# Row scatters without an order among them, and weight casts tied to the turns of a scan

## The chip, the cores and the metric

The kernel runs on one core of one Trainium2 chip. The metric is the device time of one execution in microseconds. A timed run of the kernel before gives one number; the median of three such runs is its time. A profile of one further execution shows every instruction on the engines: TensorE (PE, with its weight loads PEld), VectorE (DVE), ScalarE (ACT), GpSimd (POOL) and SyncE (SP, which here only issues DMAs).

## The reference

Two stages. The first is a gated linear attention over batch 4, 8 heads, 768 steps and head size 48, with a complex gate whose modulus is cut at 0.999:

```
scale = minimum(mag, 0.999) / (mag + 1e-06)
new_re = ar * S_re - ai * S_im;  new_im = ar * S_im + ai * S_re
S_re, S_im = new_re + kv, new_im          # kv: outer product of k[t] and v[t]
y[t] = q[t] @ S_re
```

The second takes the 3072 x 384 rows of y as tokens x of a mixture of 8 experts, of which each token uses one:

```
logits = x @ w_gate + modality_bias[modality_id]
e = argmax(logits)
out[token] = softmax(logits)[e] * (relu(x[token] @ w1[e]) @ w2[e])   # 384 -> 1024 -> 384
```

## The kernel before

**The program and its order.** The kernel is written in a layer that records instructions in program order and then places them: each engine has one queue in a fixed order, chosen by a planner that steps through a simulated time and takes, for an engine that is free, the ready instruction that comes first in the program. The layer finds dependencies by the tiles and memory ranges that an instruction reads and writes and adds the semaphore waits. On the chip each engine then works through its queue in order, so a waiting instruction holds all that stand behind it.

**The gate loop** (`gate_loop`). The 32 (batch, head) pairs are cut into 8 stretches of 96 steps, 256 rows in all, treated in two rounds `r` of 128 rows, one row a partition. For each round `elem(r)` is the scan: it walks 12 chunks `c` of 8 steps from the last (`c` = 11) to the first. In each step DVE makes the complex product of the running gate product `e` and the normed gate `an` (tile `x`, line 143) and adds its parts (line 150). Beside it `modulus` loads the gates two chunks ahead (tile `ab`, SP, lines 66 and 67) and squares them on ACT (line 69), and `hats` squares a finished chunk's `e` (line 97), scales q and k by it, transposes q on TensorE (line 111) and writes k to the scratch `kh` in HBM (line 115).
`units(r)` is the attention itself: 16 units for a round, each with a `front` (load `KW` from `kh` and `V`, memsets of V and KT on POOL in lines 170 and 173, transposes of KW in line 177, scores `wp` in line 184 and their mask on DVE), a `decay` and a `back` (products `py`, the gate logits, and the bf16 rows to `x_rows` in HBM). Round 0's scan runs alone; round 1's is woven chunk by chunk between the units of round 0; the units of round 1 run alone.

**The weight casts** (`cast_weights`). Sixteen DMAs on POOL's queue turn the experts' f32 weights into bf16 copies `w1b` and `w2b` in HBM, 768 KB of output each (lines 289 and 290). They stand before the gate loop in the program and depend on nothing.

**The expert stage** (`moe_sorted`). The tokens are sorted by expert into tiles of 256 slots by a chain of DVE operations. For each tile `fetch` loads the expert's w1 and w2 from the bf16 copies (SP, lines 444 and 445, three buffers each) and gathers 256 rows of x_rows by two indirect DMAs on POOL (line 449, six buffers); `turn` transposes them; `up` makes the first layer (line 469) with relu on DVE and ACT; `down` makes the second layer (line 481), scales it into `y_sb` (line 484 on ACT, line 486 on DVE, four buffers) and scatters the 128 rows to `out` by an indirect DMA on POOL (line 487). Twelve tiles always run; those beyond stand in Ifs on the count found on the chip. In the profiled execution 13 tiles ran, 26 gathers and 26 scatters. All scatters write to `out` at rows known only on the chip, so the layer makes each wait for the one before.

Of the kernel before, what the change touches and what calls it, by code (L numbers as in the profile page):

```python
# [13 lines left out]
Alu = mybir.AluOpType  # L14
# [5 lines left out]
ET = mybir.EngineType  # L20


def gate_loop(nc, ctx, tc, cpool, ident, identb, q, k, v, a_re, a_im, wgp, x_rows, lg):


    B, H, S, D = q.shape
# [36 lines left out]
    def modulus(r, c, box):  # L63

        ab = st.tile([P, 2, T, D], F32, name="ab", bufs=3)
        nc.sync.dma_start(out=ab[:, 0], in_=rows(a_re, r, c))
        nc.sync.dma_start(out=ab[:, 1], in_=rows(a_im, r, c))
        sq = st.tile([P, 2, T, D], F32, name="sq")
        nc.scalar.activation(sq[:], ab[:], Act.Square)
        yield  # L70
        m = st.tile([P, T, D], F32, name="m", bufs=3)
        nc.vector.tensor_tensor(m[:], sq[:, 0], sq[:, 1], Alu.add)
        nc.scalar.activation(m[:], m[:], Act.Ln, scale=1.0 / (0.999 * 0.999))
        nc.scalar.activation(m[:], m[:], Act.Exp, scale=-0.5)
        g = st.tile([P, T, D], F32, name="g")
        nc.scalar.activation(g[:], m[:], Act.Copy, scale=-1e-6 / 0.999, bias=1.0)  # L76
        yield
        nc.vector.scalar_tensor_tensor(g[:], m[:], 1.0, g[:], Alu.min, Alu.mult)
        box[c] = (ab, g)

    def gates(c, box):

        ab, g = box[c]
        an = st.tile([P, T, 4, D], F32, name="an")
        nc.vector.tensor_tensor(an[:, :, 0:2, :].rearrange("p t c d -> p c t d"), ab[:], g[:, None].broadcast_to([P, 2, T, D]), Alu.mult)
        nc.scalar.activation(an[:, :, 2, :], an[:, :, 1, :], Act.Copy, scale=-1.0)
        nc.scalar.activation(an[:, :, 3, :], an[:, :, 0, :], Act.Copy)
        box[c] = an
# [28 lines left out]
    def elem(r):  # L117

        QT = qt.tile([C, P, L], F32, name="QT", bufs=2)
        for_round[r] = QT  # L120
        last = NCH - 1
        E = {last: st.tile([P, T, 2, D], F32, name="e", bufs=3)}
        nc.vector.memset(E[last][:, T - 1, 0, :], 1.0)
        nc.vector.memset(E[last][:, T - 1, 1, :], 0.0)
        cl = un.tile([P, 2, D], F32, name="cl", bufs=1)
        box = {}
        for c in (last, last - 1):
            for _ in modulus(r, c, box):
                pass
        gates(last, box)  # L130
        for c in range(last, -2, -1):
            hs = hats(r, c + 1, E.pop(c + 1), QT) if c < last else iter(())
            ms = modulus(r, c - 2, box) if c > 1 else iter(())
            next(hs, None)
            next(ms, None)
            beside = [None, hs, ms, hs, hs, ms, hs, ms]
            if c >= 0:
                an = box.pop(c)
                if c:
                    E[c - 1] = st.tile([P, T, 2, D], F32, name="e", bufs=3)  # L140
                for i in range(T - 1, -1, -1):
                    x = st.tile([P, 2, 2, D], F32, name="x")
                    nc.vector.tensor_tensor(x[:], E[c][:, i, :, None, :].broadcast_to([P, 2, 2, D]), an[:, i].rearrange("p (u w) d -> p u w d", u=2), Alu.mult)  # L143
                    if i == T - 1:
                        if c:
                            gates(c - 1, box)
                    else:
                        next(beside[T - 1 - i], None)
                    to = E[c][:, i - 1] if i else (E[c - 1][:, T - 1] if c else cl[:])
                    nc.vector.tensor_tensor(to, x[:, 0], x[:, 1], Alu.add)  # L150
            for g in (ms, hs):
                for _ in g:
                    pass
            if c == 0:
                nc.sync.dma_start(out=c_scr[r], in_=cl.rearrange("p c d -> p (c d)"))
            yield
# [105 lines left out]
    for _ in elem(0):  # L262
        pass
    for r in range(NR):
        us = units(r)
        if r + 1 < NR:

            es = elem(r + 1)
            n, m = NB * G, NCH + 1
            done = 0  # L270
            next(es)
            for i in range(n):
                next(us)
                while done * n < (i + 1) * (m - 1):
                    next(es)
                    done += 1
            for _ in es:
                pass
        for _ in us:
            pass  # L280


def cast_weights(nc, moe_w1, moe_w2):

    E, Dt, F = moe_w1.shape
    w1b = nc.dram_tensor("w1b", (E, 128, Dt // 128, F), BF16, kind="Internal").ap()
    w2b = nc.dram_tensor("w2b", (E, 128, F // 128, Dt), BF16, kind="Internal").ap()
    for e in range(E):
        nc.gpsimd.dma_start(out=w1b[e], in_=moe_w1[e].rearrange("(k p) f -> p k f", p=128))
        nc.gpsimd.dma_start(out=w2b[e], in_=moe_w2[e].rearrange("(c p) d -> p c d", p=128))  # L290
    return w1b, w2b


def moe_sorted(nc, ctx, tc, cpool, identb, lg, x_rows, w1b, w2b, moe_modality_id, moe_modality_bias, out):

    N, Dt = out.shape
# [140 lines left out]
    ids = mp.tile([128, NH], U32, name="ids")  # L437
# [38 lines left out]
    def down(i, w2t, hT):  # L476
        for s in range(HS):
            c = i * HS + s
            y_ps = pp.tile([128, Dt], F32, name="y_ps", tag="y", bufs=2)
            for f in range(NF):  # L480
                nc.tensor.matmul(y_ps[:], hT[:, f, s * 128:(s + 1) * 128], w2t[:, f, :], start=(f == 0), stop=(f == NF - 1))  # L481
            y_sb = fp.tile([128, Dt], F32, name="y_sb", bufs=4)
            if s % 2 == 0:
                nc.scalar.activation(y_sb[:], y_ps[:], Act.Copy, scale=inv[:, 1, c:c + 1])
            else:
                nc.vector.tensor_scalar(y_sb[:], y_ps[:], inv[:, 1, c:c + 1], None, Alu.mult)  # L486
            nc.gpsimd.indirect_dma_start(out=out, out_offset=bass.IndirectOffsetOnAxis(ap=ids[:, c:c + 1], axis=0), in_=y_sb[:], in_offset=None, bounds_check=N - 1, oob_is_err=False)  # L487


    got = fetch(0)  # L490
# [1 line left out]
    for i in range(NL):  # L492
        coming = fetch(i + 1)
        hT = up(got[0], xgT)
        if i + 1 < NL:
            xgT = turn(coming[2])
        down(i, got[1], hT)
        got = coming
    nt = nc.values_load(ntile[0:1, 0:1], min_val=NL, max_val=NS, skip_runtime_bounds_check_because="N tokens in at most E tiles that are not full")  # L499
    with ExitStack() as more:  # L500
        for i in range(NL, NS):
            more.enter_context(tc.If(nt > i))
            if i > NL:
                got = fetch(i, "n")
            down(i, got[1], up(got[0], turn(got[2])))


@with_exitstack
def kernel(
    ctx: ExitStack,  # L510
    tc: tile.TileContext,
    q: bass.AP,
    k: bass.AP,
    v: bass.AP,
    a_re: bass.AP,
    a_im: bass.AP,
    moe_modality_id: bass.AP,
    moe_w_gate: bass.AP,
    moe_modality_bias: bass.AP,
    moe_w1: bass.AP,  # L520
    moe_w2: bass.AP,
    out: bass.AP,
):
    nc = tc.nc
    B, H, S, D = q.shape
    N, Dt = out.shape
    E = moe_w_gate.shape[1]
    assert Dt == H * D

    x_rows = nc.dram_tensor("x_rows", (N, Dt), BF16, kind="Internal").ap()  # L530

    cpool = ctx.enter_context(tc.tile_pool(name="c", bufs=1))
    ident = cpool.tile([128, 128], F32, name="ident")
    make_identity(nc, ident[:])
    identb = cpool.tile([128, 128], BF16, name="identb")
    nc.vector.tensor_copy(identb[:], ident[:])
    lg = cpool.tile([96, N // 96, E], F32, name="lg")

    wgp = cpool.tile([128, H // 2, 32], F32, name="wgp")
    nc.vector.memset(wgp[:], 0.0)  # L540
    for u in range(2):
        nc.sync.dma_start(out=wgp[u * 64:u * 64 + D, :, 0:E], in_=moe_w_gate.rearrange("(j u d) e -> u d j e", u=2, d=D)[u])

    w1b, w2b = cast_weights(nc, moe_w1, moe_w2)
    with ExitStack() as gstack:
        gate_loop(nc, gstack, tc, cpool, ident, identb, q, k, v, a_re, a_im, wgp, x_rows, lg)
    moe_sorted(nc, ctx, tc, cpool, identb, lg, x_rows, w1b, w2b, moe_modality_id, moe_modality_bias, out)


# [28 lines left out]
```

## Time and profile before

| | |
|---|---|
| timed runs | 612.57, 619.71, 619.93 us (median 619.71) |
| profiled execution | time 614.6 us, span 612.7 us |
| mean granted TensorE clock | 0.851 |
| PE busy | 397.7 us (65% of the span) |
| DVE busy | 354.4 us (58%) |
| ACT busy | 266.7 us (44%) |
| POOL busy | 82.7 us (13%) |
| DMA moved | 91.49 MB, mean 149 GB/s |

The span runs from the first to the last instruction of the profiled execution; its time is 1.9 us longer. The shares are means over stages: the scan of round 0 up to about 125 us, scan and units together to about 315, the units of round 1 to about 445, the sort to about 483, the experts to the end. A granted clock of 1.00 is 2.4 GHz and one of 0.50 is 1.2 GHz; means between them mix the two. A DMA share is the mean busy share of 16 DMA engines; where packets overlap it can be above 1.

### The profile page before, as it was taken

The numbers are of one execution on the slowest core, as the hardware profiler recorded it, in microseconds if no ns is written. First come the engines' busy times: TensorE is split into PE (matmuls) and PEld (weight loads), VectorE is DVE, ScalarE is ACT, GpSimd is POOL, SyncE is SP. The second block draws the span as 40 slices with busy tenths as digits, with TensorE's granted clock in tenths as the row PEclk, the third lists the DMA queues.
The fourth block names the chain that finished last, engine by engine and source line by source line (L and its number), as shares of the span: only waits on it lengthen the run. The fifth ranks groups of instructions, "written<-read, shape, count | busy, mean of one in ns | idle before, by whom it ended". The sixth has DMA issues, their size and how long they took to land. (4 is left out here: it accounts for less than half of the span.)

```text
span 612.7 us, 10055 instructions
## 1 busy us (share of the span) xinstructions
PE 397.7 (65%) x3656; PEld 292.1 (48%) x3656; DVE 354.4 (58%) x884; ACT 266.7 (44%) x597; POOL 82.7 (13%) x144
## 2 busy tenths in 40 slices
PE   0022122129799978987987999999914695876670
PEld 0011011117566656665656767776604574654450
DVE  1899999988876587588871444444365142232120
ACT  3556756475745574476652444444410031211120
POOL 5112000000000000000000000000000343435322
PEclk9999999999755685588996999999955599887886
DMA  9999998365652364353525445444217177765610
GB/s 201 234 243 267 261 254 218 116 175 117 172 151 74 93 159 127 87 154 99 134 70 114 88 93 105 91 98 99 50 12 305 32 269 254 255 230 184 206 53 28
DMA packets 108405, 91.49 MB, mean 149 GB/s; under 512 B 73342, under 2 KB 97314, under 8 KB 108352
## 3 DMA queue, kind: packets, MB, share of 16 engines
q1 hardware_dynamic: 93920, 70.94, 41.7%
q0 software_dynamic: 14432, 19.86, 15.7%
q8 instruction: 31, 0.51, 0.4%
q14 instruction: 22, 0.18, 0.1%
HBM read 86.75 MB, written 29.59 MB: 190 GB/s over the span
## 5 line engine op out<-in xcount | busy, mean ns | idle before, releaser
L111 PE MATMUL tq<-ident,Qh 128*96 128x128 f32 x192 | 42.9, 390 | 119.2 <-DVE Qh L107 119.2
L111 PEld LDWEIGHTS tq<-ident,Qh 128*96 128x96 f32 x192 | 31.3, 180 | 128.2 <-ACT g L76 62.0
L219 PE MATMUL py<-KW,V 96*64 96x192 f32 x512 | 88.9, 378 | 0.0
L185 DVE TENSOR_TENSOR KW<-wp,mask 96x384 f32<-96x384 f32 x64 | 35.3, 553 | 78.5 <-PE wp L184 67.0
L143 DVE TENSOR_TENSOR x<-e,an 128x192 f32<-128x192 f32 x192 | 67.7, 353 | 2.5
L184 PE MATMUL wp<-QT,KT 96*64 96x96 f32 x1024 | 65.8, 287 | 0.8 <-ACT KT L178 0.5
L184 PEld LDWEIGHTS wp<-QT,KT 96*64 96x64 f32 x1024 | 58.5, 165 | 5.6 <-ACT KT L178 4.3
L469 PE MATMUL h_ps<-xgT,w1t 128*128 128x256 bf16 x312 | 42.6, 296 | 25.2 <-DVE hT L471 22.0
L473 ACT ACTIVATE hT<-h_ps 128x512 bf16<-128x512 f32 x26 | 15.5, 597 | 97.5 <-PE h_ps L469 97.5
L150 DVE TENSOR_TENSOR e<-x 128x96 f32<-128x96 f32 x190 | 48.0, 253 | 2.7
L469 PEld LDWEIGHTS <-w1t 128*128 128x128 bf16 x312 | 32.8, 105 | 33.3 <-issue 26.3
L173 POOL MEMSET KT<- 96x256 f32 x32 | 10.9, 365 | 275.0 <-PE wp L184 275.0
L223 PE MATMUL py<-QT,Zs 96*48 96x96 f32 x448 | 37.5, 272 | 14.1 <-ACT Zs L209 14.1
L177 PE MATMUL tk<-ident,KW 96*96 96x96 f32 x256 | 40.1, 298 | 9.4 <-DMA KW<-kh 8.9
L219 PEld LDWEIGHTS py<-KW,V 96*64 96x64 f32 x512 | 39.6, 154 | 10.4 <-issue 2.4
L486 DVE TENSOR_SCALAR y_sb<-y_ps,inv 128x384 f32<-128x384 f32 x13 | 8.0, 617 | 60.9 <-DMA out_dram<-y_sb,ids 48.0
L112 ACT COPY QT<-tq 96x512 f32<-96x512 f32 x48 | 27.5, 582 | 34.9 <-PE tq L111 34.7
L481 PE MATMUL y_ps<-w2t,hT 128*128 128x384 bf16 x208 | 40.5, 353 | 0.0
L223 PEld LDWEIGHTS py<-QT,Zs 96*48 96x48 f32 x448 | 26.7, 136 | 26.9 <-ACT Zs L209 22.7
L209 ACT COPY Zs<-tz 96x512 f32<-96x512 f32 x28 | 16.3, 582 | 48.5 <-PE tz L207 48.5
L177 PEld LDWEIGHTS tk<-ident,KW 96*96 96x96 f32 x256 | 28.5, 154 | 17.6 <-issue 10.4
L178 ACT COPY KT<-tk 96x384 f32<-96x384 f32 x64 | 29.2, 477 | 16.9 <-PE tk L177 16.1
(120 smaller groups left out, 700.6 us busy)
## 6 DMA issues: line engine op xcount, KB each, us to landing
w1t<-w1b SPq DMA_DIRECT2D x13, 768.0 KB, 5.0
w2t<-w2b SPq DMA_DIRECT2D x13, 768.0 KB, 5.5
kh<-e SPq DMA_DIRECT2D x24, 384.0 KB, 2.9
KW<-kh SPq DMA_DIRECT2D x32, 288.0 KB, 3.7
w1b<-in_moe_w_dram POOLq DMA_DIRECT2D x8, 768.0 KB, 43.8
w2b<-in_moe_w_dram POOLq DMA_DIRECT2D x8, 768.0 KB, 46.4
cB<-c_scr SPq DMA_DIRECT2D x56, 96.0 KB, 3.4
ab<-in_a_re_dram SPq DMA_DIRECT2D x24, 192.0 KB, 5.3
```

Source lines behind the costliest of these rows:

```text
L111: nc.tensor.transpose(tp[:, i, :], Qh[:, t4 + i].rearrange("p c d -> p (c d)"), ident[:])
L112: nc.scalar.copy(QT[:, :, c * T + t4:c * T + t4 + 4], tp.rearrange("c t p -> c p t"))
L143: nc.vector.tensor_tensor(x[:], E[c][:, i, :, None, :].broadcast_to([P, 2, 2, D]), an[:, i].rearrange("p (u w) d -> p u w d", u=2), Alu.mult)
L150: nc.vector.tensor_tensor(to, x[:, 0], x[:, 1], Alu.add)
L177: nc.tensor.transpose(tp[:, i, :], KW[:, h4 + i, 0:C], ident[:L, :L])
L178: nc.scalar.copy(KT[:, h4:h4 + 4, 0:L], tp[:])
L184: nc.tensor.matmul(wp[u * 64:(u + 1) * 64, i, :], KT[:, h4 + i, u * 64:(u + 1) * 64], QT[:, p, :], start=True, stop=True)
L185: nc.vector.tensor_tensor(KW[:, h4:h4 + 4, C:], wp[0:L], mask[:, None, :].broadcast_to([L, 4, L]), Alu.mult)
L219: nc.tensor.matmul(py[u * 64:(u + 1) * 64, i, :], V[:, 2 * j + u, :], KW[:, 2 * j + u, :], start=True, stop=(g == 0))
L223: nc.tensor.matmul(py[u * 64:u * 64 + D, i, C:], Zs[:, j, u * 64:u * 64 + D], QT[:, p, :], start=False, stop=True)
L469: nc.tensor.matmul(h_ps[:, f, :], w1t[:, k, ff * 128:(ff + 1) * 128], xgT[:, k, :], start=(k == 0), stop=(k == KD - 1))
L481: nc.tensor.matmul(y_ps[:], hT[:, f, s * 128:(s + 1) * 128], w2t[:, f, :], start=(f == 0), stop=(f == NF - 1))
```

## The change

Two parts. The scatters to `out` are put into a group whose members are declared to have no dependency on each other: they write rows of different tokens. And the sixteen casts are no longer issued ahead of the gate loop; `cast_weights` hands back a list of functions, and `elem` issues one at the end of each chunk, with a semaphore wait on the chunk's last DVE add: in round 0 from the third chunk on (`c` = 9 to 0, ten casts), in round 1 from its first chunk (`c` = 11 to 6, six casts).

```
+def gate_loop(nc, ctx, tc, cpool, ident, identb, q, k, v, a_re, a_im, wgp, x_rows, lg, casts):
...
-                    nc.vector.tensor_tensor(to, x[:, 0], x[:, 1], Alu.add)
+                    done = nc.vector.tensor_tensor(to, x[:, 0], x[:, 1], Alu.add)
+
+                if casts and (r or c < last - 1):
+                    cast = casts.pop(0)()
+                    tc.add_manual_dep(cast.ins, done.ins.name, mybir.DependencyInfo(mybir.DependencyClass.Sync, mybir.DependencyReason.DATA), reason="spreads the casts over the turns")
...
+    casts = []
     for e in range(E):
-        nc.gpsimd.dma_start(out=w1b[e], in_=moe_w1[e].rearrange("(k p) f -> p k f", p=128))
-        nc.gpsimd.dma_start(out=w2b[e], in_=moe_w2[e].rearrange("(c p) d -> p c d", p=128))
-    return w1b, w2b
+        casts.append(lambda e=e: nc.gpsimd.dma_start(out=w1b[e], in_=moe_w1[e].rearrange("(k p) f -> p k f", p=128)))
+        casts.append(lambda e=e: nc.gpsimd.dma_start(out=w2b[e], in_=moe_w2[e].rearrange("(c p) d -> p c d", p=128)))
+    return w1b, w2b, casts
...
-            nc.gpsimd.indirect_dma_start(out=out, out_offset=bass.IndirectOffsetOnAxis(ap=ids[:, c:c + 1], axis=0), in_=y_sb[:], in_offset=None, bounds_check=N - 1, oob_is_err=False)
+
+            sc = nc.gpsimd.indirect_dma_start(out=out, out_offset=bass.IndirectOffsetOnAxis(ap=ids[:, c:c + 1], axis=0), in_=y_sb[:], in_offset=None, bounds_check=N - 1, oob_is_err=False)
+            tc.declare_no_dep(sc.ins, group="scatter", reason="rows of different tokens")
+            tc.add_to_no_dep_group("scatter", sc.ins)
...
-    w1b, w2b = cast_weights(nc, moe_w1, moe_w2)
+    w1b, w2b, casts = cast_weights(nc, moe_w1, moe_w2)
     with ExitStack() as gstack:
-        gate_loop(nc, gstack, tc, cpool, ident, identb, q, k, v, a_re, a_im, wgp, x_rows, lg)
+        gate_loop(nc, gstack, tc, cpool, ident, identb, q, k, v, a_re, a_im, wgp, x_rows, lg, casts)
```

## Rows read from the trace of the kernel before

**Rows 1.** The page's 40 slices of the span: TensorE's granted clock and DMA share, tenths.
```profile
PEclk9999999999755685588996999999955599887886
DMA  9999998365652364353525445444217177765610
```

**Rows 2.** Groups of instructions: busy, mean ns, idle before them and its releasers.
```profile
L487 POOL DMA_INDIRECT out_dram<-y_sb,ids x26 | 25.9, 994 | 66.0 <-DMA out_dram<-y_sb,ids 30.9 <-issue 13.6 <-DVE xgT L459 10.2
L449 POOL DMA_INDIRECT xg<-x_rows,idg x26 | 25.3, 972 | 44.9 <-DVE empty L436 37.2 <-issue 4.9 <-PE y_ps L481 1.2
L486 DVE TENSOR_SCALAR y_sb<-y_ps,inv 128x384 f32<-128x384 f32 x13 | 8.0, 617 | 60.9 <-DMA out_dram<-y_sb,ids 48.0 <-PE y_ps L481 10.1 <-PE h_ps L469 2.8
```

**Rows 3.** Timeline of POOL, expert stage: start, length, instruction, idle before it.
```profile
541.89 1.00 POOL L487 DMA_INDIRECT out_dram<-y_sb,ids  x1 [2.43 <-DVE xgT L459]
...
546.07 1.01 POOL L487 DMA_INDIRECT out_dram<-y_sb,ids  x1 [0.61 <-issue]
551.22 1.00 POOL L487 DMA_INDIRECT out_dram<-y_sb,ids  x1 [4.15 <-DMA out_dram<-y_sb,ids]
```

**Rows 4.** Timeline of TensorE: the first layer of tiles 1, 3 and 11.
```profile
495.15 2.78 PE L469 MATMUL h_ps<-xgT,w1t 128*128 128x256 bf16 x24
...
506.26 3.04 PE L469 MATMUL h_ps<-xgT,w1t 128*128 128x256 bf16 x24
...
581.78 2.88 PE L469 MATMUL h_ps<-xgT,w1t 128*128 128x256 bf16 x24
```

**Rows 5.** Timeline of the end, all engines.
```profile
597.56 0.62 DVE L486 TENSOR_SCALAR y_sb<-y_ps,inv 128x384 f32<-128x384 f32 x1 [2.56 <-PE y_ps L481]
...
606.49 0.97 POOL L487 DMA_INDIRECT out_dram<-y_sb,ids  x1 [1.94 <-DMA out_dram<-y_sb,ids]
```

**Rows 6.** Timeline of ACT, round 0: one square of e a chunk.
```profile
23.84 0.84 ACT L97 ACTIVATE sqe<-e 128x768 f32<-128x768 f32 x1 [4.08 <-DVE e L150]
...
44.48 0.84 ACT L97 ACTIVATE sqe<-e 128x768 f32<-128x768 f32 x1 [1.35 <-DVE e L150]
...
109.06 0.84 ACT L97 ACTIVATE sqe<-e 128x768 f32<-128x768 f32 x1 [1.35 <-DVE e L150]
```

**Rows 7.** Timeline of the start, all engines.
```profile
13.59 0.84 ACT L69 ACTIVATE sq<-ab 128x768 f32<-128x768 f32 x1 [1.03 <-DMA ab<-in_a_im_dram]
...
18.71 0.35 DVE L143 TENSOR_TENSOR x<-e,an 128x192 f32<-128x192 f32 x1
```

**Rows 8.** Tile ab (the gate loads): its transfers from issue to landing.
```profile
DMA to landing us min/median/max: 2.4/5.5/9.0
```

**Rows 9.** Windows: busy us of PE, PEld, DVE, ACT, POOL; clock, DMA share, GB/s.
```profile
497.00:502.00 5.00, 5.00 (x43) 3.75 (x41) 2.25 (x4) 1.44 (x3) 0.00 (x0) 1.00 0.93 325
502.00:507.00 5.00, 5.00 (x43) 3.75 (x42) 1.56 (x3) 1.77 (x3) 2.96 (x3) 1.00 0.92 345
```

**Rows 10.** Timeline of POOL: the last of the 16 weight casts.
```profile
53.44 0.84 POOL L290 DMA_DIRECT2D w2b<-in_moe_w_dram  x1 [6.66 <-DMA w2b<-in_moe_w_dram]
```

**Rows 11.** Timeline of the middle stage, all engines, and one more row of POOL.
```profile
173.21 0.20 POOL L170 MEMSET V<- 96x128 f32 x1 [3.83 <-PE py L219]
...
173.54 0.54 SPq L169 DMA_DIRECT2D KW<-kh  x1
...
178.47 1.73 PE L177 MATMUL tk<-ident,KW 96*96 96x96 f32 x8
...
187.20 0.20 POOL L170 MEMSET V<- 96x128 f32 x1 [3.78 <-PE py L219]
```

**Rows 12.** SP's waits: line, releaser: us in total, times, longest.
```profile
SPq L171 <- POOL V L170: 8.1, 29, 0.3
```

**Rows 13.** DMA issues: count, KB each, median us to landing.
```profile
KW<-kh SPq DMA_DIRECT2D x32, 288.0 KB, 3.7
```

**Rows 14.** Windows of the middle stage, columns as in rows 9.
```profile
180.00:200.00 20.00, 18.66 (x154) 13.83 (x152) 12.79 (x37) 9.59 (x23) 0.82 (x3) 0.50 0.38 105
300.00:320.00 20.00, 18.18 (x207) 12.25 (x206) 15.56 (x44) 11.94 (x29) 1.02 (x4) 1.00 0.33 83
```

More of the change, by code (lines that the diff above doesn't have):

```diff
@@ L20 @@
 ET = mybir.EngineType
-def gate_loop(nc, ctx, tc, cpool, ident, identb, q, k, v, a_re, a_im, wgp, x_rows, lg):
+def gate_loop(nc, ctx, tc, cpool, ident, identb, q, k, v, a_re, a_im, wgp, x_rows, lg, casts):
     B, H, S, D = q.shape
```

## The prediction

> **What bounds the kernel now.** I read the profile from the end backwards. The rows of slices (15.3 us each) [rows 1] show the stages: DMA at eight tenths or more for the first 107 us, a middle stage in which TensorE's clock falls, and a last quarter in which DMA is seldom above seven tenths. That last quarter is the expert stage, and the groups [rows 2] say what it waits for: the 26 row scatters are idle 66.0 us before their issue, the longest part released by an earlier scatter, and the DVE copy that fills a scatter's buffer is idle 48.0 us for the same reason. The issue of a scatter or a gather costs POOL 0.99 or 0.97 us, so its four issues of one tile are 3.9 us of work. The timeline of POOL [rows 3] shows the pattern: 541.89, 546.07, 551.22. Two scatters and two gathers take 9.33 us, though little of it is busy: each scatter stands in POOL's queue until the one before has landed, the gathers stand behind it, and four y_sb buffers run out. TensorE shows the pace without that [rows 4]: its first matmuls of tiles 1 and 3 start at 495.15 and 506.26, 5.56 us for a tile, while the scatter chain was not yet full; tile 11 starts at 581.78, ten tiles after the first, which is 8.66 us each. At the end [rows 5] the last y_sb is written at 597.56 + 0.62 = 598.18 and its scatter is issued only at 606.49: 8.3 us in which POOL works off a backlog alone. So the expert stage is bound by the order among scatters.
>
> The first stage, the scan of round 0, runs alone. From the fourth chunk on it is bound by DVE, whatever the casts do: the squares of e, one for each finished chunk, each wait for DVE and start 9.23 us apart (44.48 to 109.06, seven chunks) [rows 6], with DMA full. Only its start feels the casts: the third chunk's a_im is squared at 13.59, after a DMA wait, and the first scan product starts at 18.71 [rows 7]; loads of ab land in 2.4 us at best and 9.0 us at worst [rows 8].
>
> **Part one, the scatters.** The change takes away the wait of each scatter for the one before. y_sb still waits for the scatter four earlier, which at 5.56 us a tile was issued two tiles before, 11 us; a landing is some 2.4 us by POOL's waits [rows 3], so that wait goes. What is late next is TensorE: tile 11 would start at 495.15 + 10 x 5.56 = 550.7 in place of 581.78, which gives 31.1 us. POOL's 3.9 us of issue a tile, with some 0.3 us after each, fit under 5.56. At the end the backlog goes (8.3 us, less the 0.2 us in which a scatter follows its y_sb): 8.1 us. Sum 39.2 us at TensorE's pace.
>
> The unknown is DMA. A tile moves two weights of 128 x 3072 bf16 (1.573 MB), two gathers of 128 x 384 bf16 (0.197 MB) and two scatters of 128 x 384 f32 (0.393 MB): 2.163 MB. In 5.56 us that is 389 GB/s, and the fullest stretches show 345 and 325 GB/s at a DMA share of 0.92 and 0.93 [rows 9]. At 345 a tile takes 6.27 us, 0.71 too long; over the ten tiles fetched in the loop 7.1 us. Against it stands a lead: three weight buffers, so a load may take two tiles, 11.1 us. Taking the median landing of the gate loads, 5.5 us [rows 8], as an estimate for a weight load, 5.6 us of lead can be eaten first. Left over: 1.5 us at 345 GB/s; at 325 (6.66 us a tile) 11.0 - 5.6 = 5.4 us. I take 2, since 345 is the nearer to what the hardware was asked for. Part one: 39.2 - 2 = **37 us** (34 to 39).
>
> The Trainium skill's page "DMA: Bandwidth & Descriptors", section Specifications, puts the HBM limit of a core at about 358 GB/s, which speaks against a free run: by it an estimate of 6.04 us a tile, more than TensorE's 5.56, so DMA would set the pace. The rows at 325 and 345 agree with such a ceiling, and by 358 the lead would cover the excess (4.8 us) whole and the sum would be 39 in place of 37.
>
> **Part two, the casts.** All 16 stand at the front of POOL's queue now; eight go out at once and the rest each wait for an earlier one to land, the last at 53.44 after 6.66 us of wait [rows 10]. After the change ten are issued in round 0, one after each chunk from the third on, and six in round 1.
> What it gives: the start. If the third a_im lands in 2.4 instead of up to 9.0 us, 6.6 us; in the median 5.5, 3.5 us [rows 8]. I take 5, since the loads still compete with each other. Then the first two intervals of the chunks, 23.84 to 44.48, are 20.64 us where two at 9.23 are 18.45: 2.2 us more [rows 6]. Together **7.2 us** (5 to 9). In the rest of round 0 a cast every 9.2 us meets a scan that ran at DVE's pace beside a denser stream, so I cost it at nothing; its cover is that loads are issued about two chunks ahead, and if that failed each chunk could lose what the second lost, 2 us.
> What it costs: in round 1 the scan runs beside the units. A cast now waits for DVE's last add of a chunk, and behind it on POOL stand the memsets of V and KT. The loads of V wait for their memset, 29 times [rows 12], KW is queued behind V on SP, and TensorE transposes KW: memset 173.21, KW 173.54, transpose 178.47 [rows 11]. KW lands in 3.7 us [rows 13], so it is there at 177.2 to 177.8 and has about 1 us of slack. No row shows a KW load beside a cast. Bounds: at 5.5 us, the median of ab, it is 1.8 later, 0.8 beyond the slack; at 9.0, 4.3 beyond. A cast lasts some 6.7 us [rows 10] of a unit of 14.0 us (memsets of V at 173.21 and 187.20 [rows 11]), so it meets about every second load: six casts, three to six late loads, 2 to 26 us; nothing in that stage is removed, so no gain. I take 6, near the lower end, as ab's median was itself taken beside casts for half its loads. The issue of a cast, 0.84 us, delays a memset at most six times: 1 us. Cost **7 us** (2 to 27).
>
> **The sum.** 37 + 7.2 - 7 = 37. The profiled execution has a span of 612.7 us and a time of 614.6, so 614.6 - 37 = **577.6, say 578 us**. The three timed runs are 612.57, 619.71 and 619.93: the profiled one stands near the lowest, 5 us under the median, and if the changed kernel lies the same way its median could be 583. I keep 578 and put the 5 us into the range. A change under 2% could not be told from none here.
>
> **Rivals.**
> DMA sets the expert stage's pace. For it: the row at 345 GB/s is below the 389 needed, and scatters that overlap take DMA share from the weights. Against it: the lead of two tiles. With the stage at 286 GB/s, the lower of what I hold possible (an estimate, 12% under 325), a tile takes 7.56 us: 20 - 5.6 = 14 us lost where I counted 2, 590 us.
> The clock of the middle stage comes out otherwise. From 180 to 200 us TensorE did 154 matmuls at a granted clock of 0.50, from 300 to 320 it did 207 at 1.00 [rows 14], the two levels 1.2 and 2.4 GHz. The digits of the clock from 153 to 291 us [rows 1] make some 100 us at the lower level. If these ran at the upper one, 100 x (1 - 154/207) = 26 us go, 552 us; if the rest of the stage, some 55 us, fell to the lower one, 55 x (207/154 - 1) = 19 us come, 597 us. Shifted work and casts can do either.
> The scatters keep an order, because something else orders them (a shared semaphore, an index read, the If around the last tile). Then only 7.2 - 7 is left: 614 us, no change. Against it: the gathers, on the same queue and of the same kind, have, beyond the 37.2 us for the sort, 7.7 us of idle time before 25 issues [rows 2], 0.3 us each.
> Slower than before: each cast holds POOL, and through V, SP's queue and so KW. If a cast stands ahead of memsets whose unit comes before the end of its chunk, it holds them as long as DVE is late. A hold of a whole unit is 14.0 us, six of them 84: 614.6 - 44 + 84 = 655 us. It decides once a hold is above 44/6 = 7.3 us each. Against it: memsets are ready early, and DVE, which ends the chunk, also takes the units' products in its own fixed order.
>
> **How the numbers follow.** Forecast as summed, with its unknown costs: 0.62. DMA pace 0.14. Clock, either way, 0.14. Scatters still ordered 0.06. Casts hold POOL 0.04. The range runs from 561 to 598: below, half of what a better clock gives; above, the larger DMA and clock costs. It leaves out the last two and half the clock's fast side, about 0.17. Faster by over 2% (under 607): 0.62 + 0.14 + 0.14 = 0.90; no change 0.06; slower 0.04.
>
> **What would show it.** Right: scatters on POOL issued 1.3 us apart or as y_sb comes, no DMA in front of y_sb, TensorE's tiles 5.6 to 6.3 us apart, no backlog after the last y_sb; the first scan product at 12 to 15 us and chunks at 9.2 from the start; casts on POOL at the chunk ends. Wrong: tiles at 7 us or more with DMA share near one, waits of a transpose for KW or of SP for a memset of V beside casts, or a granted clock in the middle stage far from that of before.

## The result, and the profile after

The changed kernel takes 582.01 us in the median of four runs (578.42 to 582.48), the kernel before beside it 619.82 us (612.57 to 621.01). The ratio is 0.94, with a 95% interval of 0.933 to 0.947. The profiled execution took 581.57 us, its span is 579.9 us. A later set of the same kernel gave a median of 570.9 us against 617.9 us, ratio 0.926 (0.920 to 0.931). The forecast of 578 us lies between the two. Executions more than 1.5% above the fastest of the same kernel in their set belong to a slower state, and the times and ratios in this text leave them out unless they are named.

Behind the scan the line numbers of the kernel after are four to six higher: the KW transposes are L181, py from KW and V is L223, the gather L454, the first layer L474, the second L486, the DVE copy into y_sb L491, the scatter L493.

**The scatters.** The page of the kernel after, first TensorE's granted clock and DMA share in 40 slices of 14.5 us, then the start of the chain that ended last:

```profile
PEclk9999999999999697585559959999999755799998
DMA  6359989998499699354233623554442180599960
...
PE 12%; issue 1%; DMA 1%; POOL 0%; POOLq 0%; DVE 0%
```

The end is now TensorE's: 12% of the span lead back through its matmuls. The same is seen in the groups of the expert stage (busy, mean ns of one, idle before and its releasers), which answer to [rows 2]:

```profile
L493 POOL DMA_INDIRECT out_dram<-y_sb,ids x26 | 25.8, 990 | 21.2 <-ACT y_sb L489 9.8 <-ACTq L508 4.9 <-issue 4.9
L491 DVE TENSOR_SCALAR y_sb<-y_ps,inv 128x384 f32<-128x384 f32 x13 | 8.0, 618 | 27.6 <-PE y_ps L486 27.6
```

In this trace no scatter and no y_sb waits for an earlier scatter any more (30.9 and 48.0 us before); both wait for what feeds them. (In a second trace of the same kernel one y_sb waits 2.0 us for a scatter's landing.) POOL's timeline shows the two scatters and two gathers of a tile 1.3 to 1.7 us apart, against [rows 3]:

```profile
508.88 1.00 POOL L493 DMA_INDIRECT out_dram<-y_sb,ids  x1 [0.30 <-issue]
510.19 1.00 POOL L493 DMA_INDIRECT out_dram<-y_sb,ids  x1 [0.30 <-issue]
511.87 0.99 POOL L454 DMA_INDIRECT xg<-x_rows,idg  x1 [0.68 <-PE xg_ps L462]
513.16 0.96 POOL L454 DMA_INDIRECT xg<-x_rows,idg  x1 [0.30 <-PE y_ps L486]
```

TensorE's timeline gives the pace, tiles 1, 2, 3 and 11 here against [rows 4]: 5.56 us from tile to tile, and (558.63 - 503.08) / 10 = 5.56 over all ten.

```profile
503.08 2.78 PE L474 MATMUL h_ps<-xgT,w1t 128*128 128x256 bf16 x24
508.64 2.78 PE L474 MATMUL h_ps<-xgT,w1t 128*128 128x256 bf16 x24
514.20 2.78 PE L474 MATMUL h_ps<-xgT,w1t 128*128 128x256 bf16 x24
...
558.63 2.78 PE L474 MATMUL h_ps<-xgT,w1t 128*128 128x256 bf16 x24
```

The timeline of the end, against [rows 5]: the last y_sb is written at 570.92 + 0.62 = 571.54 and its scatter goes out 0.58 us later, not 8.3.

```profile
570.92 0.62 DVE L491 TENSOR_SCALAR y_sb<-y_ps,inv 128x384 f32<-128x384 f32 x1 [2.56 <-PE y_ps L486]
572.12 0.97 POOL L493 DMA_INDIRECT out_dram<-y_sb,ids  x1 [0.30 <-issue]
```

**The casts.** ACT's squares of e in round 0, against [rows 6], and POOL's first cast (timelines):

```profile
18.59 0.84 ACT L97 ACTIVATE sqe<-e 128x768 f32<-128x768 f32 x1 [4.08 <-DVE e L150]
...
37.43 0.84 ACT L97 ACTIVATE sqe<-e 128x768 f32<-128x768 f32 x1 [1.35 <-DVE e L150]
...
101.98 0.84 ACT L97 ACTIVATE sqe<-e 128x768 f32<-128x768 f32 x1 [1.35 <-DVE e L150]
```
```profile
38.40 0.93 POOL L294 DMA_DIRECT2D w1b<-in_moe_w_dram  x1 [36.03 <-DVE e L150]
```

The first square comes 5.25 us earlier, the third 7.05, and from there the chunks are 9.22 us apart beside the spread casts, as they were before (9.23).

**The span cut in three.** Start: to chunk 0's square in round 0. Middle: from there to the first gather. Expert stage: from the first gather to the end of the span. All from timelines, in us:

| trace | start | middle | experts | span |
|---|---|---|---|---|
| before | 125.24 | 357.51 | 129.95 | 612.7 |
| after | 118.53 | 371.26 | 90.11 | 579.9 |
| difference | -6.71 | +13.75 | -39.84 | -32.8 |

So two terms came about as forecast (-39.84 for -37, -6.71 for -7.2) and the third looks twice as dear (+13.75 for +7). The experiments ask whether the casts are its cause.

### The profile page after: what moved, and what is told of

It is laid out like the page before. It is cut to its first block, busy times and chain, and to the rows that moved or that the text cites. A ratio compares the mean times of both kernels' runs of the same rounds, so it can differ in the third digit from the quotient of the medians.

```text
span 579.9 us, 10062 instructions
## 1 busy us (share of the span) xinstructions
PE 401.0 (69%) x3656; PEld 297.1 (51%) x3656; DVE 355.9 (61%) x884; ACT 267.5 (46%) x597; POOL 81.5 (14%) x144
## 5 line engine op out<-in xcount | busy, mean ns | idle before, releaser
L111 PE MATMUL tq<-ident,Qh 128*96 128x128 f32 x192 | 43.8, 397 | 112.1 <-DVE Qh L107 112.1
L223 PE MATMUL py<-KW,V 96*64 96x192 f32 x512 | 94.5, 401 | 0.0
L111 PEld LDWEIGHTS tq<-ident,Qh 128*96 128x96 f32 x192 | 32.4, 185 | 121.1 <-ACT g L76 62.0
L189 DVE TENSOR_TENSOR KW<-wp,mask 96x384 f32<-96x384 f32 x64 | 35.4, 553 | 84.6 <-PE wp L188 83.3
L188 PE MATMUL wp<-QT,KT 96*64 96x96 f32 x1024 | 68.8, 297 | 0.6 <-ACT KT L182 0.3
L188 PEld LDWEIGHTS wp<-QT,KT 96*64 96x64 f32 x1024 | 61.2, 172 | 5.6 <-ACT KT L182 3.9
L227 PE MATMUL py<-QT,Zs 96*48 96x96 f32 x448 | 38.8, 280 | 13.9 <-ACT Zs L213 13.9
L223 PEld LDWEIGHTS py<-KW,V 96*64 96x64 f32 x512 | 42.4, 164 | 11.4 <-issue 2.7
L181 PE MATMUL tk<-ident,KW 96*96 96x96 f32 x256 | 40.2, 298 | 11.0 <-DMA KW<-kh 10.1
L474 PE MATMUL h_ps<-xgT,w1t 128*128 128x256 bf16 x312 | 38.4, 283 | 1.1 <-DVE xgT L464 1.1
L181 PEld LDWEIGHTS tk<-ident,KW 96*96 96x96 f32 x256 | 28.6, 155 | 19.2 <-issue 12.1
L486 PE MATMUL y_ps<-w2t,hT 128*128 128x384 bf16 x208 | 35.9, 326 | 0.0
L233 ACT COPY yT<-py 128x192 f32<-128x192 f32 x64 | 20.3, 318 | 33.0 <-DVE state L232 27.8
L474 PEld LDWEIGHTS <-w1t 128*128 128x128 bf16 x312 | 31.6, 101 | 7.1 <-issue 1.3
```

Source lines behind the costliest of these rows:

```text
L111: nc.tensor.transpose(tp[:, i, :], Qh[:, t4 + i].rearrange("p c d -> p (c d)"), ident[:])
L181: nc.tensor.transpose(tp[:, i, :], KW[:, h4 + i, 0:C], ident[:L, :L])
L188: nc.tensor.matmul(wp[u * 64:(u + 1) * 64, i, :], KT[:, h4 + i, u * 64:(u + 1) * 64], QT[:, p, :], start=True, stop=True)
L189: nc.vector.tensor_tensor(KW[:, h4:h4 + 4, C:], wp[0:L], mask[:, None, :].broadcast_to([L, 4, L]), Alu.mult)
L223: nc.tensor.matmul(py[u * 64:(u + 1) * 64, i, :], V[:, 2 * j + u, :], KW[:, 2 * j + u, :], start=True, stop=(g == 0))
L227: nc.tensor.matmul(py[u * 64:u * 64 + D, i, C:], Zs[:, j, u * 64:u * 64 + D], QT[:, p, :], start=False, stop=True)
```

## The experiments

Two explanations stand against each other. Theory: the scatters give the expert stage's gain, the moved casts the start's; the middle is longer because of the casts beside the units. Rival: the middle varies by itself, with TensorE's pace, and the casts cost next to nothing there. The first four kernels take the parts one by one and move the casts out of round 1.

**Scatters alone.** The casts stand at the front again:

```
-    w1b, w2b, casts = cast_weights(nc, moe_w1, moe_w2)
+    w1b, w2b, casts = cast_weights(nc, moe_w1, moe_w2); casts = [cast() for cast in casts][:0]
```

> The changed kernel with all 16 casts issued at the front again; only the order among the scatters is gone. My theory (the scatters give some 39 us; the casts give 7 us at the start and pay about as much back beside the units of round 0): the expert stage as in the changed kernel, first gather to end about 90 us, and 578 to 584 us in all, within 1% of the changed kernel. Rival A (the casts give their 7 us net and the loss of 10 us in the middle stage was only a clock that fell earlier): 587 to 591. Rival B (the casts cost more than they give): 572 to 577.

Measured: 580.44 and 582.57 us (left out: 591.83 and 599.1), profiled 582.57. Start 125.76, middle 360.1, experts 94.7 us. The scatter gain is there without the casts, the start's is not.

**Casts alone.** The dependency among the scatters stays:

```
-            tc.declare_no_dep(sc.ins, group="scatter", reason="rows of different tokens")
-            tc.add_to_no_dep_group("scatter", sc.ins)
```

> The changed kernel with the order among the scatters put back; only the casts are moved. My theory: no change against before, 616 to 623, with the scan's first chunk done 5 us and its third 7 us earlier, and that lead gone again when round 1's scan ends. Rival A (the lead stays): 611 to 614. Rival B (casts cost net): 625 to 630.

Measured: 603.21 and 608.27 us (left out: 624.17 and 629.64), profiled 608.27. Start 119.05, middle 355.4, experts 131.8. The start is won and, against the expectation, stays won; the expert stage is as before. And the middle, whose instructions are those of the kernel after, takes 355.4 us where that took 371.3.

**All casts in round 0.** Two after each of the chunks 9 to 4, one after each of 3 to 0:

```
-                if casts and (r or c < last - 1):
-                    cast = casts.pop(0)()
+                for cast in [casts.pop(0)() for _ in range(0 if r or c >= last - 1 else 2 if c > 3 else 1)]:
```

> The changed kernel with all 16 casts in round 0 (two after each of the chunks 9 to 4, one after each of 3 to 0), none beside the units. If the casts beside the units take back the lead (my theory): the lead of 7 us at the end of round 0's scan lives through the middle stage, 573 to 577. If the clock alone took it (rival A): no better than the changed kernel, 580 to 584. If denser casts slow the scan of round 0 (rival C): its chunks are over 9.3 us apart while two casts are in flight, and 584 or more.

Measured: 579.33 and 579.43 us (left out: 591.14 and 593.14), profiled 579.43. Start 121.55 (chunk 0's square is 2 to 3 us late), middle 361.4, experts 94.6. No cast is issued beside a unit, and the middle is not the shortest.

**All casts at the end of chunk 9.**

```
+                for cast in [casts.pop(0)() for _ in range(16 if not r and c == last - 2 else 0)]:
```

> The changed kernel with all 16 casts tied to one point, the end of chunk 9 of round 0; not spread. If only the start matters and the scan is bound by its vector engine even beside full DMA, as the trace of before showed: as the run with all casts in round 0, 573 to 577, chunks 9.2 us apart. If the spreading is what protects the scan's loads: chunks of 10 us or more for some 70 us, 582 to 590.

Measured: 579.96 us in the median of three (575.55 to 580.97), ratio 0.935 (0.926 to 0.943). The profiled execution is the one left out, 588.77 us: start 121.28, middle 371.4, experts 94.4. That one execution shows only that a middle as long as the longest can come with no cast beside a unit; with the second trace of the kernel after, below, the theory that casts beside units make it long falls. The chunks are 9.22 us apart here too, from the third on, and chunk 0's square is 2 to 3 us late as with all casts in round 0. So what the start needs is that the casts stand behind the scan's first loads; up to chunk 1 (111.19 us, 110.49 in the kernel after) it matters little whether they are spread.

**All casts in round 1**, the reverse:

```
+                for cast in [casts.pop(0)() for _ in range(0 if not r else 2 if c > last - 4 else 1)]:
```

> The kernel after, with no cast in the first pass over the queries and keys and all sixteen in the second: two after each of its first four scan chunks, one after each of the other eight. It tests the third term of the prediction, that casts beside the attention units cost 7 us (late loads of kh for KW, POOL's time for issuing). If that term is right, sixteen casts beside units instead of six cost 7 x 16/6 = 19 us: the square of chunk 0 in the second pass (318.6 in the profile after) comes 10 to 12 us later, the run takes 590 to 596 us. Theory formed on the traces so far: a cast beside units costs the wait of KW's product 1 us in all; the start still comes 7 us early, the first stage is undisturbed, and the run takes 575 to 586 us, like the kernel after, with the length from chunk 0's square to the first gather anywhere from 355 to 372 us, by the duration of the py matmuls (374 to 401 ns) and not by the casts.

Measured: 580.14 us in the median of three (578.42 to 581.14), ratio 0.945 (0.938 to 0.951). Start 118.42, middle 362.8, experts 95.3. Sixteen casts beside the units, and the middle lies within the spread of the others. The wait of the transposes of KW for its load, whole run, by the groups of the kernels before, after and this one:

```profile
L177 PE MATMUL tk<-ident,KW 96*96 96x96 f32 x256 | 40.1, 298 | 9.4 <-DMA KW<-kh 8.9 <-ACT QT L112 0.5
```
```profile
L181 PE MATMUL tk<-ident,KW 96*96 96x96 f32 x256 | 40.2, 298 | 11.0 <-DMA KW<-kh 10.1 <-ACT QT L112 0.9
```
```profile
L181 PE MATMUL tk<-ident,KW 96*96 96x96 f32 x256 | 39.8, 298 | 11.2 <-DMA KW<-kh 10.3 <-ACT QT L112 0.7
```

8.9 us with no cast beside a unit (8.9 to 9.6 over the four traces with the casts in front), 10.1 with six (10.1 to 10.8 over six traces), 10.3 with sixteen: the direct cost is about 1 us. Nearly all of it lies in two loads, the first after the scan of round 0 and one about the end of round 1's scan (timelines, before and after):

```profile
138.80 1.49 PE L177 MATMUL tk<-ident,KW 96*96 96x96 f32 x8 [6.66 <-DMA KW<-kh]
327.99 1.49 PE L177 MATMUL tk<-ident,KW 96*96 96x96 f32 x8 [2.28 <-DMA KW<-kh]
```
```profile
133.13 1.49 PE L181 MATMUL tk<-ident,KW 96*96 96x96 f32 x8 [7.69 <-DMA KW<-kh]
331.38 0.84 PE L181 MATMUL tk<-ident,KW 96*96 96x96 f32 x8 [2.37 <-DMA KW<-kh]
```

The second load differs by 0.1 us, and the loads between them, beside the six casts, cost TensorE nothing. With sixteen casts the two waits are 6.51 and 3.83 us. (With all casts in round 0, at chunks 9 to 0 or at once, the sum is 13.2 and 13.4 us, because the first load alone waits 10.8 and 11.0; why, I did not follow up.)

**The kernel after, again**, unchanged:

> The kernel after once more, unchanged, in five rounds beside the kernel before and beside the kernel with the free scatters alone. Two things are open. First the part from the square of chunk 0 of the first pass to the first gather: 371.3 us in the first trace, 355.4 with the very same instructions when the scatters were still ordered. If this is TensorE's pace and not the program, a second trace gives another value between 355 and 372 us and the mean duration of the py matmuls goes with it (374 to 401 ns); if it is the program, 371 us and 401 ns again. Second the expert stage: tiles 5.56 us apart and 90.1 us in all in the first trace, 94.5 us in three variants whose instructions there are the same. If it is the program, 90.1 again; if it is the single execution, either may come. Time 578 to 583 us.

Measured: 570.9 us in the median of five (567.84 to 576.11; left out: 585.95), below the expected time. Profiled 572.02: start 119.45, middle 355.6, experts 95.1. The same program now has a middle 15.7 us shorter and an expert stage 5 us longer: both expectations for "not the program" came true. The two traces come from two sets, and whether the chip was the same is not on record, so "the execution" may in part be "the chip".

**Scatters alone, again**, beside it:

> The free scatters alone once more (casts at the front as in the kernel before), beside the kernel after on the same chip, so that the net worth of the moved casts is seen with less scatter. By the prediction's terms: the start gains 7.2 us, the middle loses 7, net nothing, both kernels the same within 2 us. By the theory on the traces so far (7 us won at the start, 1 us lost beside the units): this kernel takes 5 to 7 us longer than the kernel after. By the rival that the casts in the middle lower TensorE's pace (13 us lost there): this kernel is 5 to 7 us faster than the kernel after.

Measured: 578.1 us in the median of four (572.96 to 581.13; left out: 584.69 and 592.75), ratio to before 0.937 (0.930 to 0.944). Profiled 576.01: start 124.92, middle 355.05, experts 94.0. By the medians the moved casts are worth 7 us here; in the two traces, 574.0 - 570.1 = 3.9 us: 5.5 from the start, less 0.5 in the middle and 1.1 in the expert stage. The intervals of the two ratios overlap a little, so by times alone the size is loose, and a worth as small as the 2 us that the expectation allowed for "the same" is not excluded. Times and traces both point the same way, against the prediction's net of nothing and against the rival that the casts lower the pace (this kernel faster).

**The kernel before, again**, blank lines added:

> The kernel before once more (blank lines added so that its line numbers are those of the kernel after; instructions and their order are the same). By the reading that the middle of the program varies with TensorE's pace and the rest does not: the first scan chunk's square at 23.5 to 24.2 us and chunk 0's at 124.9 to 125.8, the first gather 355 to 372 us after that, with the mean of the py matmuls at 374 to 401 ns, and the expert stage from the first gather 128 to 132 us. The rival, that the kernel before has a middle of its own (357.5 us), would give 357 to 358 us again.

Measured: 629.92 us (one run), span 627.8. Start 125.36, middle 369.3, experts 133.15 (1 us over what was expected). So the kernel before has a long middle too.

What makes the middle long is TensorE's pace. Mean duration of a py matmul and middle, trace by trace: 374 ns, 355.05 (scatters alone again) and 355.4 (casts alone); 375, 355.6 (after again); 378, 357.5 (before); 378, 362.8 (all in round 1); 384, 361.4 (all in round 0); 386, 361.7 (two weight buffers, below); 387, 360.1 (scatters alone); 394, 371.4 (all at chunk 9); 396, 369.3 (before again); 401, 371.3 (after). One group is a rough measure. TensorE's whole busy time over the middle says it better (windows with the columns of [rows 9], the first and the second trace of the kernel after):

```profile
118.53:489.79 371.26, 304.36 (x2970) 224.68 (x2970) 217.10 (x552) 173.75 (x430) 21.64 (x73) 0.82 0.54 124
```
```profile
119.45:475.00 355.55, 286.41 (x2970) 213.00 (x2970) 216.47 (x552) 172.54 (x430) 21.64 (x72) 0.83 0.56 129
```

The same 2970 matmuls are busy for 304.36 and 286.41 us, while TensorE is idle for 66.9 and 69.1 us. Over all thirteen traces of this text the idle time of the middle stays between 65.4 and 71.8 us, with no cast, six or sixteen beside the units; the busy time goes from 286.3 to 304.4. A stretch of the kernel after shows it closer, by a window and by the py group of that window; the same two views of its second trace follow:

```profile
147.00:154.00 7.00, 7.00 (x38) 4.38 (x36) 1.25 (x6) 3.97 (x11) 0.20 (x1) 1.00 0.30 96
```
```profile
L223 PE MATMUL py<-KW,V 96*64 96x192 f32 x14 | 3.4, 550 | 0.0
```
```profile
144.00:150.00 6.00, 6.00 (x57) 3.67 (x54) 5.20 (x14) 4.63 (x16) 0.40 (x2) 1.00 0.55 152
```
```profile
L223 PE MATMUL py<-KW,V 96*64 96x192 f32 x25 | 3.6, 347 | 0.0
```

TensorE is busy throughout in both, with 38 matmuls in 7 us and 57 in 6 us. A py matmul takes 550 and 347 ns. In the kernel before the same group takes 536 ns from 180 to 200 us, at a granted clock of 0.50, and 341 ns from 300 to 320 at 1.00 [rows 14] (groups of these two windows):

```profile
L219 PE MATMUL py<-KW,V 96*64 96x192 f32 x24 | 5.2, 536 | 0.0
```
```profile
L219 PE MATMUL py<-KW,V 96*64 96x192 f32 x40 | 7.4, 341 | 0.0
```

By its durations the first stretch ran at the lower level, 1.2 GHz, though its record says 1.00. It is not alone in that: the transposes of q in the scan of round 0 (tq, L111) take 421 ns in both traces at a recorded 1.00, and 272 to 283 ns later. So the pace does not fall early in the first trace, it rises late. In the second trace the durations become the short ones at 143 us, after TensorE had been busy without a gap from 134; in the first they do so only at about 180 us, though it had been busy without a gap from 133 to 160. The 15.7 us between the two middles are all lost by round 1's chunk 7, whose square comes 84.6 and 68.9 us after round 0's chunk 0. Why the pace rises later in one execution than in another of the same program stays open.

**Two weight buffers instead of three**, for the question why a full DMA costs nothing:

```
+        w1t = fp.tile([128, KD, F], BF16, name="w1t" + n, bufs=2)
+        w2t = fp.tile([128, NF, Dt], BF16, name="w2t" + n, bufs=2)
```

> The kernel after, with two buffers instead of three for each of the two weight tiles of an expert (bufs=2); the order on every engine is that of the kernel after. It tests whether the transfers, which in the expert stage of the kernel after run at a DMA share of 1.0 and land 7.3 us (up to 10.7) after their issue, cost nothing because a weight load is asked for two tiles (11.1 us) before it is read. Theory: with two buffers a load can only be asked for when the expert before last has been multiplied, one tile or 5.56 us ahead; it lands 5 to 7.3 us later, so TensorE waits 0 to 2 us for weights in each of 12 tiles and the expert stage goes from 90.1 to 95 to 115 us, with waits of TensorE named after the weight loads. Rival: the loads follow the traffic and land in 5 us as in the kernel before; then tiles stay 5.56 us apart and the stage stays at 90 to 95 us.

Measured: 577.88 us (one run), experts 94.7 us, as with three buffers, and no wait of TensorE for weights: the rival holds. The lead that a third buffer gives, on which the prediction counted, was not needed: here a load of w1t is issued some 8.3 us before its first use (498.32 for the tile at 506.64), and that is enough.

**Less traffic.** In most traces of kernels with free scatters the expert stage takes 94 to 95 us, not 90.1, because most tiles are about 6.05 us apart. This kernel leaves out twelve of the thirteen loads of w1t and computes every tile with the w1 of the first tile's expert:

```
+        w1t = fp.tile([128, KD, F], BF16, name="w1t") if i == 0 else got[0]
+        if i == 0: nc.sync.dma_start(out=w1t[:], in_=w1b[bass.ds(te, 1)].rearrange("e p k f -> p (e k) f"))
```

> The kernel after, but w1t is loaded once, for the first tile of experts, and used by all of them: nine of ten 768 KB loads are left out, and the output is that of the first expert's w1 everywhere. Per tile 1.38 MB move instead of 2.16. Open is why, in six of seven traces of kernels with free scatters, most tiles are 6.05 us apart and TensorE waits for the third quarter of hT, where TensorE's own work is 5.56 us (the first trace of the kernel after has 5.56 throughout). Theory: the traffic does it, whatever the last wait is called; 2.16 MB per 6.05 us is 357 GB/s. Then with 1.38 MB the tiles are 5.55 to 5.6 us apart nearly throughout and the expert stage takes 90 to 91 us. Rival: it is not the traffic (TensorE's signals or VectorE come late for another reason); then most tiles stay at 6.0 to 6.1 us and the stage at 94 to 95 us.

> The same kernel a second time (w1t loaded once), since one trace in seven had 5.56 us with the full traffic: by the traffic theory 5.55 to 5.6 us again and a stage of 90 to 91 us, by the rival tiles of 6.05 us in at least one of the two traces.

Measured: 576.27 and 578.41 us. TensorE's timeline and a window of the first (columns as in [rows 9]):

```profile
504.58 2.78 PE L474 MATMUL h_ps<-xgT,w1t 128*128 128x256 bf16 x24
510.72 2.78 PE L474 MATMUL h_ps<-xgT,w1t 128*128 128x256 bf16 x24
```
```profile
505.00:525.00 20.00, 18.79 (x155) 13.93 (x154) 8.49 (x14) 5.35 (x10) 13.13 (x14) 1.00 0.75 218
```

Tiles 6.14 us apart at 218 GB/s, and 95.8 and 95.6 us for the stage: it is not the traffic. The trace of the first kernel with free scatters shows where the half microsecond goes (timeline of one tile):

```profile
505.18 2.78 PE L474 MATMUL h_ps<-xgT,w1t 128*128 128x256 bf16 x24
506.10 0.69 DVE L476 TENSOR_SCALAR hT<-h_ps 128x512 bf16<-128x512 f32 x1
506.74 0.60 ACT L478 ACTIVATE hT<-h_ps 128x512 bf16<-128x512 f32 x1 [2.08 <-PE h_ps L474]
508.94 0.69 DVE L476 TENSOR_SCALAR hT<-h_ps 128x512 bf16<-128x512 f32 x1 [2.16 <-PE xg_ps L462]
509.02 0.60 ACT L478 ACTIVATE hT<-h_ps 128x512 bf16<-128x512 f32 x1 [1.68 <-PE xg_ps L462]
509.69 2.12 PE L486 MATMUL y_ps<-w2t,hT 128*128 128x384 bf16 x12 [0.74 <-DVE hT L476]
```

The third quarter of h_ps is recorded as multiplied in time (24 matmuls in 2.78 us), but DVE takes it up only 3.76 us after the tile's start, and TensorE then waits 0.74 us for it. In the first trace of the kernel after, DVE takes the third quarter 2.17 us after the start (508.64 to 510.81). In the late tile ACT takes the fourth quarter at 509.02, released by TensorE's transposes (L462) just as DVE is, so it is TensorE's results or their signals that come late and not DVE alone. What delays them stays open: neither the program (the same one shows both), nor the number of weight buffers, nor the traffic of the weights.

## Why the prediction was right, point by point

**What bounds.** Right. Taking away the order among scatters alone removes the wait, and the stage runs at TensorE's pace, but for the half microsecond a tile that stays open above.

**Part one, 37 us.** Right in its mechanism; that the size agrees so closely is in part luck. The terms in the first trace: tile 11 comes 68.84 us after the first gather instead of 99.03, 30.2 us for 31.1, as tile 0 took 0.8 us longer; from tile 11 to the end 21.27 us instead of 30.92, 9.65 for 8.1. Together 39.84. Over all traces with the reference's work the stage takes 129.95, 131.8 and 133.15 us with ordered scatters and 90.1 to 95.3, median 94.65, without: 131.8 - 94.65 = 37.2 us. In the second trace of the kernel after the two terms are 25.2 for 31.1 and 9.7 for 8.1: the late uptake, which the prediction did not have, takes about 5 us; the 2 us set aside for DMA, which DMA did not take, and 1.6 us more at the end stand against it. One reading was wrong without harm: the 2.4 us that I took for a landing [rows 3] is a wait for DVE's xgT; the wait for a scatter in the same rows is 4.15 us, and the median landing 3.2 before and 6.8 after, still under the 11 us of the argument. A full stretch of the kernel after, by windows:

```profile
500.00:520.00 20.00, 20.00 (x164) 14.96 (x163) 8.49 (x15) 6.50 (x11) 13.71 (x15) 1.00 0.92 325
520.00:540.00 20.00, 20.00 (x172) 15.59 (x170) 10.06 (x16) 6.52 (x11) 14.18 (x15) 1.00 1.02 391
```

DMA moved the 389 GB/s that I said a tile needs; the 325 and 345 of before [rows 9] were what was asked for there, not a ceiling. Landings grew (weights from 5.0 to 7.3 us, scatters from 3.2 to 6.8) and TensorE waited for no weight. The Trainium skill's figure of about 358 GB/s a core ("DMA: Bandwidth & Descriptors", Specifications) does not hold here as a limit: 391 GB/s were moved for 20 us. That most tiles take 6.05 us, near the estimate of 6.04 by that figure, is chance, as 1.38 MB a tile takes 6.14.

**Part two, the start, 7.2 us.** Right: 6.7 in the first pair, and right in its parts. The third a_im is squared at 8.44 us without a wait and the first scan product starts at 13.47, against 13.59 and 18.71 [rows 7]: 5.2 for the 5 forecast. The first two intervals of the chunks are 18.84 us, 1.8 less for the 2.2; by chunk 0 some 0.3 us are gone again. Chunk 0's square comes at 118.4 to 119.6 us in five traces (after twice, casts alone, two buffers, all in round 1), against 124.9 to 125.8 in the four with the casts in front: 5.3 to 7.3 us. The transfers of ab land in 2.4/4.2/8.1 us (shortest, median, longest) against 2.4/5.5/9.0 [rows 8].

**Part two, the cost, 7 us.** Mis-sized: it is about 1 us. The step that failed is "six casts, three to six late loads" beyond 1 us of slack. Loads of KW land in 3.9 us in the median, 0.2 over [rows 13], and TensorE waits for none of those beside the six casts; the 1 us is the first load after round 0's scan, 7.69 for 6.66 us. SP's wait for the memsets of V is 8.1 us, 29 times, as in [rows 12]: the 1 us that I gave POOL's issue is nothing.

**The sum.** With the cost at 1 us the terms give a gain of 37.2 + 6.7 - 1 = 43 us. The first set measured 37.8 (619.82 to 582.01), the second 47.0 (617.9 to 570.9), so they stand about 5 us to either side. The first set's profiled execution had a long middle, which the kernel before has in other executions too (of the set's other runs there is no trace). The forecast lay right in part by luck: a cost that is not there stood about where the clock's spread lies. A slip in the range: its low end, 561, is called half of what a better clock gives, which from 578 and 552 is 565.

**The rivals.** DMA as the pace: not seen (above). The clock of the middle stage: this is the one that acts, with 355 to 371 us, but in both kernels, so it widens the interval and does not make the difference. The rival was priced by the granted clock of the record, which stands at 1.00 for the first 140 us although TensorE's matmuls there take the durations of the lower level. Scatters still ordered, casts that hold POOL: not seen; POOL's chunk-end waits hold nobody.

## What to carry to other kernels

When indirect scatters go to rows that cannot meet, declare them free of each other: in order each costs its issue and its landing, 1.0 and 3.2 us in the median here, and two of them, 8.4 us, are near the 8.66 us that a tile took; the gathers queued behind them on POOL and the output buffers that ran out carry the wait to TensorE. Before a stage's change is put down to an edit, look at a second trace of the same program; here the middle stage differed by 16 us between two. And when an edit adds traffic, price it by the waits that it adds where the data is needed, not by its landing time.

## What the runs showed of the hardware

DMA reached 391 GB/s over 20 us, at a share of 1.02. The granted clock in the record can say 1.00 where matmuls take what they take at 0.50: py 550 against 347 ns, with 536 at a recorded 0.50, and the transposes of q 421 ns all through the scan of round 0. After the scan the short durations came at 143 us in one trace and at about 180 in another of the same program. So the same program with the same data has a middle stage of 355.6 or 371.3 us. And in the expert stage the results of TensorE can be taken up 1.6 us late (3.76 against 2.17 us after a tile's start) with no gap in its own record; in seven of the eight traces with free scatters and all weight loads, six to eight of ten tiles are 5.96 us or more apart.
